# A softmax sum with half the products, and a multiply split between VectorE and Pool, in a four-layer attention kernel

## The chip, the core and the metric

The kernel runs on one core of one Trainium2 chip. The metric is the time of one launch on the device, in microseconds (us). PE is the matrix engine, VectorE (DVE in the profile), ScalarE (ACT) and Pool (POOL) are the three others that compute. SP issues most of the DMA transfers. Engines wait for each other through semaphores: counters that one engine raises when it has done something, and that another waits for. "Granted clock" is the share of its full clock that PE was given.

## The reference, cut to what matters

Four layers run one after the other, A, B, A, B. Layer A is a segmented attention that the change does not touch. Layer B is a recurrent one. It walks over 64 segments of 32 tokens, and each segment starts with 8 memory tokens that the segment before it produced, so no step can start before the step before it has ended.

```python
def _B_ref(x, mem0, Wq, Wk, Wv, Wo, seg_len):      # 2048 tokens, width 640, 32 heads of 128
    mask = (idx[:, None] < M) | (idx[:, None] >= idx[None, :])
    mem = mem0                                     # M = 8 memory tokens
    for s in range(n_seg):                         # 64 segments
        h = jnp.concatenate([mem, xs], axis=1)     # 8 + 32 = 40 tokens
        q, k, v = ...                              # three projections of h
        scores = jnp.where(mask, q @ k * scale, -1e9)
        p = _softmax(scores, axis=-1)
        o = (p @ v) @ Wo
        mem = o[:, :M, :]                          # the next step needs this
        outs.append(o[:, M:, :])
```

## The kernel before

A step s of layer B is one pass through the code below; `i4 = s % 4`. Work on heads is done in two halves b = 0 and 1, 16 heads each. The 40 keys of a head are split in two groups: 32 keys (8 older tokens and 24 of the segment), and 8 "tail" keys. A score tile holds, for each of four heads r, 56 columns: 16 columns for the tail keys (only the last 16 queries may see them) and 40 columns for the 32 keys and all 40 queries. All engines run their instructions in program order.

```python
def alloc_h(s):                                    # called for s + 1 at the start of step s
    hT[s] = hp.tile([128, NCH, 56], BF16, name="b_hT", tag="hT")
    nc.gpsimd.tensor_copy(hT[s][:, :, 0:24], xcols(s, 0, 24))         # by Pool, a step ahead
    nc.gpsimd.tensor_copy(hT[s][:, :, 32:56], xcols(s + 1, 0, 24))    # by Pool
    # ...columns 24:32, the memory tokens, come from VectorE at the end of step s - 1

def scores(b):
    t = SP[b] = ps_tile([128, 512], F32, "b_SP")
    # ...4 mask products, then 32 score products (KT is the weight, QT is streamed)
    nc.scalar.activation(out=PT[:, b]..., in_=t[:, 0:224], func=ACT.Exp, scale=SCB, **acc)

def sums(b):                                       # blk holds ones: a product with it adds over keys
    sm_ = SP[b][:, 256:480].rearrange("p (r c) -> p r c", c=56)
    for k in range(2):
        for part in range(2):
            for j in range(4):
                c0, c1 = ((16, 56), (40, 56))[k] if part == 0 else (0, 16)
                rhs = PT[:, b, :, 0:16] if k else PT[:, b, :, 40:56] if part else PT[:, b, :, 16:56]
                nc.tensor.matmul(sm_[32 * j:32 * j + 32, :, c0:c1], lhsT=blk[:, k, j],
                                 rhs=rhs, start=(k == 0 and part == 0), stop=(k == 1), ...)

def normalise(b):
    R = wk.tile([128, 4, 56], F32, name="b_R", tag="R")
    flat = R[:].rearrange("p r c -> p (r c)")
    nc.scalar.activation(out=flat, in_=SP[b][:, 256:480], func=ACT.Ln)
    nc.scalar.activation(out=flat, in_=flat, func=ACT.Exp, scale=-1.0)      # 1 / sum
    nc.vector.tensor_tensor(out=PT[:, b], in0=PT[:, b], in1=R[:], op=ALU.mult)
    if not general:
        nc.gpsimd.tensor_tensor(out=Rtot[:], in0=Rtot[:], in1=R[:, :, 16:56], op=ALU.add)
```

The order of a step, as PE gets it (`V0` and `V1` are the projections of the values, 5 parts of 4 products each; `fill` puts in products of the next tile of four segments, or deferred output products, for about so many us; `op` is the output projection):

```python
qk(Q, 0); qk(K, 0); qk(Q, 1); K1.run(2)
scores(0)
K1.run(3)
if i4 == 0 and T + 1 < NT: tail_cols(T + 1)        # Pool copies b_hx
V0.run(1); sums(0); normalise(0); V0.run(4)
scores(1)
V1.run(3)
values(0)                                          # 32 products b_OTL, weights b_Vsb and b_Vt, PT streamed
V1.run(2); sums(1)
take("act", 0, 0); take("act", 0, 1)               # ScalarE casts b_OTL to b_OTsb
normalise(1)
op.run(4); op.run(4)                               # b_OPS
fill(0.44)
values(1)
fill(0.66)
take("dve", 1, 0); take("act", 1, 1)
op.run(8)
# ...Pool copies b_OTdef; VectorE turns b_OPS into b_TM and adds it into b_hT of the next step
```

Of the kernel before, what the change touches and what calls it, by code (L numbers as in the profile page):

```python
# [18 lines left out]
F32 = mybir.dt.float32  # L19
BF16 = mybir.dt.bfloat16  # L20
ACT = mybir.ActivationFunctionType
ALU = mybir.AluOpType
# [565 lines left out]
def layer_B(nc, tc, C, W, wo_src, x_src, xb_src, x_dst, mem0, general, nsteps=64, out_bf16=False):  # L588
# [3 lines left out]
    nc = _OrdNC(tc, nc_raw, engines=ORDER_ENGINES)  # L592
    assert nsteps % 4 == 0
    NT = nsteps // 4
    with ExitStack() as ctx:
# [3 lines left out]
        wk = st  # L599
# [15 lines left out]
        blk = st.tile([128, 2, 4, 32], BF16, name="b_blk")  # L615
# [4 lines left out]
        if not general:  # L620
            Rtot = st.tile([128, 4, 40], BF16, name="b_Rtot")
# [249 lines left out]
        for s in range(nsteps):  # L871
# [32 lines left out]
            PT = wk.tile([128, 2, 4, 56], BF16, name="b_PT", tag="PT")  # L904
# [5 lines left out]
            SP = {}  # L910
# [72 lines left out]

            def sums(b):

                sm_ = SP[b][:, 256:480].rearrange("p (r c) -> p r c", c=56)
                for k in range(2):
                    for part in range(2):
                        for j in range(4):
                            c0, c1 = ((16, 56), (40, 56))[k] if part == 0 else (0, 16)  # L990
                            rhs = PT[:, b, :, 0:16] if k else PT[:, b, :, 40:56] if part else PT[:, b, :, 16:56]
                            nc.tensor.matmul(sm_[32 * j:32 * j + 32, :, c0:c1], lhsT=blk[:, k, j],
                                             rhs=rhs, start=(k == 0 and part == 0), stop=(k == 1),
                                             tile_position=(0, 32 * j), skip_group_check=True)

            def normalise(b):

                R = wk.tile([128, 4, 56], F32, name="b_R", tag="R")
                flat = R[:].rearrange("p r c -> p (r c)")
                nc.scalar.activation(out=flat, in_=SP[b][:, 256:480], func=ACT.Ln)  # L1000
                nc.scalar.activation(out=flat, in_=flat, func=ACT.Exp, scale=-1.0)
                nc.vector.tensor_tensor(out=PT[:, b], in0=PT[:, b], in1=R[:], op=ALU.mult)
                if not general:
                    nc.gpsimd.tensor_tensor(out=Rtot[:], in0=Rtot[:], in1=R[:, :, 16:56], op=ALU.add)

            def values(b):
                for jp in range(2):
# [40 lines left out]
            V0 = VPass(0)  # L1048
            V0.run(1)
            sums(0)  # L1050
            normalise(0)
            V0.run(4)
            if general:
# [10 lines left out]
            if g_need < NT:  # L1064
                ln_norm(g_need)
            V1.run(2)
            sums(1)
            take("act", 0, 0)
            take("act", 0, 1)
            normalise(1)  # L1070
            if g_need < NT:
                ln_apply(g_need)
# [3 lines left out]
            op = OPass(lambda h: OTsb[:, h, 0:32], HORDER, "b_OPS", po, "op")  # L1076
# [18 lines left out]
            if not last:  # L1095
                TM = wk.tile([128, 10, 32], F32, name="b_TM", tag="TM")
                nc.vector.transpose(out=TM[:].rearrange("p g t -> p (g t)"), in_=ops[:])
                for hf in range(2):
                    nc.vector.tensor_tensor(out=hT[s + 1][64 * hf:64 * hf + 64, :, 24:32], in0=TM[0:64, hf:10:2, 24:32],
                                            in1=TM[64:128, hf:10:2, 24:32], op=ALU.add)  # L1100
# [129 lines left out]
```

## Time and profile before

| | before |
|---|---|
| time, median of 3 runs (lowest to highest) | 2479.77 us (2478.43 to 2483.33) |
| span of the profiled run | 2479.6 us |
| PE busy | 2268.0 us, 91% |
| VectorE, Pool, ScalarE busy | 1584.5, 1014.1, 975.4 us |
| one step of layer B, median for i4 = 0, 1, 2, 3 | 13.11, 13.05, 13.30, 13.63 us |

First come lines of the page of the kernel before: the span, the busy time and number of instructions of each engine, and the DMA queue by which PE's instructions are fetched (packets, MB, share of 16 DMA engines).

```profile
span 2479.6 us, 127703 instructions
...
PE 2268.0 (91%) x57036; PEld 1309.4 (53%) x57036; DVE 1584.5 (64%) x3643; ACT 975.4 (39%) x2195; POOL 1014.1 (41%) x2333
...
q8 instruction: 448, 7.34, 1.3%
```

PE is nearly always busy, so what counts is the little time in which it is not. 448 packets with 7.34 MB are 16,384 bytes each. PE executes about 114,000 instructions here (57,036 products and as many weight loads), and 256 instructions to a packet account for nearly all the packets, so this queue is PE's.

Next, from the list of what PE waited for in the kernel before: total us, times, the longest. The list has only waits of over 150 ns, so it doesn't count every join. The word "issue" means that the profile shows nothing that PE waited for.

```profile
PE b_Qa L91 <- DVE b_hT L91: 19.5, 62, 1.2
...
PE b_OTL L91 <- issue: 5.1, 14, 0.6
...
PE b_OPSd L91 <- issue: 3.1, 6, 0.9
```

All lines say L91, because one helper records nearly every instruction; go by the names of tiles. The first line is the join between steps: PE waits for VectorE's addition into `b_hT`. The other two are waits in the midst of a group of equal products.

The timeline of the kernel before, second half of one step and the start of the next (start in us, duration in us, engine, instruction, number; in brackets the idle time before it and what ended it):

```profile
1015.92 0.39 DVE L91 TENSOR_TENSOR b_PT<-b_PT,b_R 128x224 bf16<-128x224 bf16 x1 [0.34 <-ACT b_R L91]
...
1016.03 0.63 POOL L91 TENSOR_TENSOR b_Rtot<-b_Rtot,b_R 128x160 bf16<-128x160 bf16 x1 [2.16 <-ACT b_R L91]
...
1019.29 0.40 POOL L91 COPY b_OTdef<-b_OTsb 128x256 bf16<-128x256 bf16 x1
1019.44 0.52 DVE L91 TENSOR_TENSOR b_hT<-b_TM 64x40 bf16<-64x40 f32 x2
...
1020.08 1.01 PEld L91 LDWEIGHTS <-b_hT 128*32 128x32 bf16 x24 [0.66 <-POOL b_OTdef L91]
1020.11 1.26 PE L91 MATMUL b_Qa<-b_wq,b_hT 128*32 128x512 bf16 x20 [0.20 <-DVE b_hT L91]
```

VectorE's multiply of `b_PT` ends at 1016.31. Pool's addition of `b_Rtot` starts beside it and ends at 1016.66. At the end of the step, VectorE finishes `b_hT` at 1019.96 and PE's first product of the next step starts at 1020.11.

### The profile page before, as it was taken

To read this page: it belongs to the slowest core of one execution; us is meant where nothing else is said; L and a number is where in the kernel's file an instruction comes from. 1 tells how busy PE (TensorE), PEld (TensorE's weight loads), DVE (VectorE), ACT (ScalarE), POOL (GpSimd) and SP (SyncE) were. 2 spreads that over 40 slices of the span, in tenths; PEclk is the share of its full clock that TensorE was granted. 3 is DMA by queue.
4 is the path that set the end of the run, shared out by engine and by line. 5 is a ranking of instruction groups with operands and counts; after the bars stand their busy time and mean duration, and the time that the engine had idled before them with its cause. 6 is when DMAs were issued, how large, how long until landed. Compare 5 with 4: busy or idle time off the path is not lost. (4 is left out here: it accounts for less than half of the span.)

```text
span 2479.6 us, 127703 instructions
## 1 busy us (share of the span) xinstructions
PE 2268.0 (91%) x57036; PEld 1309.4 (53%) x57036; DVE 1584.5 (64%) x3643; ACT 975.4 (39%) x2195; POOL 1014.1 (41%) x2333
## 2 busy tenths in 40 slices
PE   6888979999999999999868789699999999999997
PEld 3444435565655555556534444355555555555554
DVE  5666646666666666666556666466666666666665
ACT  4656633333333333333246566333333333333322
POOL 2334434444444444444323344344444444444442
PEclk9988979999999999999978889899999999999999
DMA  6563340111101011110032343400100000000000
GB/s 182 136 175 123 103 137 20 25 26 24 26 22 25 23 25 24 26 23 20 20 100 84 95 127 107 148 19 22 23 21 23 21 20 22 22 22 22 17 19 16
DMA packets 98864, 132.11 MB, mean 53 GB/s; under 512 B 20592, under 2 KB 84096, under 8 KB 96384
## 3 DMA queue, kind: packets, MB, share of 16 engines
q1 hardware_dynamic: 96704, 122.20, 18.2%
q8 instruction: 448, 7.34, 1.3%
q10 hardware_dynamic: 1600, 1.66, 0.2%
q14 instruction: 112, 0.92, 0.1%
HBM read 89.17 MB, written 26.21 MB: 47 GB/s over the span
## 5 line engine op out<-in xcount | busy, mean ns | idle before, releaser
L91 PEld LDWEIGHTS <-b_hT 128*32 128x32 bf16 x15520 | 409.2, 96 | 329.4 <-issue 43.3
L91 ACT ACTIVATE b_PT<-b_SP 128x224 bf16<-128x224 f32 x256 | 92.2, 360 | 789.6 <-PE b_SP L91 768.2
L91 PE MATMUL b_V<-b_wv,b_hT 128*32 128x512 bf16 x5120 | 371.2, 381 | 0.8 <-issue 0.5
L91 ACT ACTIVATE a_PT<-a_S 128x768 bf16<-128x768 f32 (+1 forms) x384 | 325.4, 892 | 80.8 <-PE a_S L91 72.4
L91 PE MATMUL b_OPS<-b_wo,b_OTsb 128*32 128x320 bf16 x8192 | 329.5, 300 | 5.4 <-DVE b_OTsb L91 5.3
L91 POOL TENSOR_TENSOR b_Rtot<-b_Rtot,b_R 128x160 bf16<-128x160 bf16 x256 | 158.0, 617 | 268.7 <-ACT b_R L91 268.4
L91 PEld LDWEIGHTS <-b_OTsb 128*32 128x32 bf16 x8192 | 200.4, 96 | 96.5 <-DVE b_OTsb L91 45.2
L91 POOL CAST b_QT<-b_TQ 128x384 bf16<-128x384 f32 x254 | 140.7, 554 | 255.4 <-DVE b_TQ L91 255.4
L91 ACT CAST b_OTsb<-b_OTL 128x320 bf16<-128x320 f32 x384 | 150.9, 428 | 217.0 <-PE b_OTL L91 188.0
L91 POOL CAST b_KT<-b_TQ 128x384 bf16<-128x384 f32 x254 | 142.6, 562 | 167.1 <-DVE b_TQ L91 167.1
L91 POOL TENSOR_SCALAR_AFFINE_SELECT a_PT<-a_PT 128x256 bf16<-128x256 bf16 x256 | 109.5, 432 | 214.7 <-ACT a_PT L91 203.5
L91 PE MATMUL b_Kb<-b_wk,b_hT 128*32 128x512 bf16 x2560 | 187.3, 381 | 0.0
L91 PE MATMUL b_Qa<-b_wq,b_hT 128*32 128x512 bf16 x2560 | 164.1, 384 | 22.7 <-DVE b_hT L91 19.5
L91 PE MATMUL b_Ka<-b_wk,b_hT 128*32 128x512 bf16 x2560 | 164.9, 384 | 0.0
L91 PE MATMUL a_PP<-a_xnT,a_wt 128*128 128x512 bf16 x560 | 160.2, 423 | 2.9 <-DVE a_t1k L91 0.8
L91 PE MATMUL b_Qb<-b_wq,b_hT 128*32 128x512 bf16 x2560 | 162.6, 380 | 0.0
L91 DVE TENSOR_TENSOR b_PT<-b_PT,b_R 128x224 bf16<-128x224 bf16 x256 | 101.8, 398 | 85.2 <-ACT b_R L91 84.9
L91 PE MATMUL a_S<-a_qk 32*128 32x512 bf16 (+3 forms) x1024 | 143.4, 322 | 7.7 <-ACT a_PT L91 6.4
L91 DVE STREAM_TRANSPOSE b_TQ<-b_Qa 128x512 f32<-128x512 f32 x128 | 91.7, 717 | 78.2 <-PE b_Qa L91 36.1
L91 DVE STREAM_TRANSPOSE b_TM<-b_OPS 128x320 f32<-128x320 f32 x126 | 65.1, 517 | 119.2 <-PE b_OPS L91 119.2
L91 DVE CAST a_qk<-a_PP 128x512 bf16<-128x512 f32 x128 | 88.0, 687 | 74.3 <-PE a_PP L91 74.3
L91 PEld LDWEIGHTS <-b_hx 128*32 128x32 bf16 x3840 | 99.6, 97 | 66.5 <-issue 10.0
(162 smaller groups left out, 4105.9 us busy)
## 6 DMA issues: line engine op xcount, KB each, us to landing
a_wt<-a_wpad SPq DMA_DIRECT2D x112, 160.0 KB
b_wo<-in_B_Wo_dram SPq DMA_DIRECT2D x8, 1280.0 KB
b_Vt<-b_Vtb SPq DMA_DIRECT2D x512, 16.0 KB
b_XO<-xres SPq DMA_DIRECT2D x256, 30.0 KB
a_wvo<-in_A_wo_dram SPq DMA_DIRECT2D x8, 800.0 KB
b_wq<-in_B_Wq_dram SPq DMA_DIRECT2D x20, 256.0 KB
b_wk<-in_B_Wk_dram SPq DMA_DIRECT2D x20, 256.0 KB
xres<-a_xo SPq DMA_DIRECT2D x16, 320.0 KB
```

What stands on the lines that cost most here:

```text
L91: r = f(*a, **k)
```

## The change

Its intent: the sum over the keys is the same for each query, whether its weight sits in the 40 columns of the 32 keys or in the 16 columns of the tail keys. The kernel before computes it twice for the last 16 queries (16 products, 352 streamed columns in each of four column groups). The change computes it once for each of the 40 queries (8 products, 224 columns) and uses the last 16 results for both. ScalarE's Ln and Exp get 160 columns instead of 224, VectorE multiplies 160 columns instead of 224, and a new multiply on Pool does the 64 tail columns beside it.

```diff
             def sums(b):
-                sm_ = SP[b][:, 256:480].rearrange("p (r c) -> p r c", c=56)
+                sm_ = SP[b][:, 256:416].rearrange("p (r c) -> p r c", c=40)
                 for k in range(2):
-                    for part in range(2):
-                        for j in range(4):
-                            c0, c1 = ((16, 56), (40, 56))[k] if part == 0 else (0, 16)
-                            rhs = PT[:, b, :, 0:16] if k else PT[:, b, :, 40:56] if part else PT[:, b, :, 16:56]
-                            nc.tensor.matmul(sm_[32 * j:32 * j + 32, :, c0:c1], lhsT=blk[:, k, j],
-                                             rhs=rhs, start=(k == 0 and part == 0), stop=(k == 1), ...)
+                    for j in range(4):
+                        nc.tensor.matmul(sm_[32 * j:32 * j + 32, :, 24 * k:40], lhsT=blk[:, k, j],
+                                         rhs=PT[:, b, :, 0:16] if k else PT[:, b, :, 16:56], start=(k == 0), stop=(k == 1), ...)

             def normalise(b):
-                R = wk.tile([128, 4, 56], F32, name="b_R", tag="R")
+                R = (wk if general else sm).tile([128, 4, 40], F32, name="b_R", tag="R")
                 flat = R[:].rearrange("p r c -> p (r c)")
-                nc.scalar.activation(out=flat, in_=SP[b][:, 256:480], func=ACT.Ln)
+                nc.scalar.activation(out=flat, in_=SP[b][:, 256:416], func=ACT.Ln)
                 nc.scalar.activation(out=flat, in_=flat, func=ACT.Exp, scale=-1.0)
-                nc.vector.tensor_tensor(out=PT[:, b], in0=PT[:, b], in1=R[:], op=ALU.mult)
+                nc.vector.tensor_tensor(out=PT[:, b, :, 16:56], in0=PT[:, b, :, 16:56], in1=R[:], op=ALU.mult)
+                nc.gpsimd.tensor_tensor(out=PT[:, b, :, 0:16], in0=PT[:, b, :, 0:16], in1=R[:, :, 24:40], op=ALU.mult)
                 if not general:
-                    nc.gpsimd.tensor_tensor(out=Rtot[:], in0=Rtot[:], in1=R[:, :, 16:56], op=ALU.add)
+                    nc.gpsimd.tensor_tensor(out=Rtot[:], in0=Rtot[:], in1=R[:], op=ALU.add)
```

(Arguments that are the same on both sides are cut as `...`. `sm` is a pool with two buffers where `wk` has one.)

More of the change, by code (lines that the diff above doesn't have):

```diff
@@ L984, in sums @@
             def sums(b):
-                sm_ = SP[b][:, 256:480].rearrange("p (r c) -> p r c", c=56)
+                sm_ = SP[b][:, 256:416].rearrange("p (r c) -> p r c", c=40)
                 for k in range(2):
-                    for part in range(2):
-                        for j in range(4):
-                            c0, c1 = ((16, 56), (40, 56))[k] if part == 0 else (0, 16)
-                            rhs = PT[:, b, :, 0:16] if k else PT[:, b, :, 40:56] if part else PT[:, b, :, 16:56]
-                            nc.tensor.matmul(sm_[32 * j:32 * j + 32, :, c0:c1], lhsT=blk[:, k, j],
-                                             rhs=rhs, start=(k == 0 and part == 0), stop=(k == 1),
-                                             tile_position=(0, 32 * j), skip_group_check=True)
+                    for j in range(4):
+                        nc.tensor.matmul(sm_[32 * j:32 * j + 32, :, 24 * k:40], lhsT=blk[:, k, j],
+                                         rhs=PT[:, b, :, 0:16] if k else PT[:, b, :, 16:56], start=(k == 0), stop=(k == 1),
+                                         tile_position=(0, 32 * j), skip_group_check=True)
             def normalise(b):
-                R = wk.tile([128, 4, 56], F32, name="b_R", tag="R")
+                R = (wk if general else sm).tile([128, 4, 40], F32, name="b_R", tag="R")
                 flat = R[:].rearrange("p r c -> p (r c)")
-                nc.scalar.activation(out=flat, in_=SP[b][:, 256:480], func=ACT.Ln)
+                nc.scalar.activation(out=flat, in_=SP[b][:, 256:416], func=ACT.Ln)
                 nc.scalar.activation(out=flat, in_=flat, func=ACT.Exp, scale=-1.0)
-                nc.vector.tensor_tensor(out=PT[:, b], in0=PT[:, b], in1=R[:], op=ALU.mult)
+                nc.vector.tensor_tensor(out=PT[:, b, :, 16:56], in0=PT[:, b, :, 16:56], in1=R[:], op=ALU.mult)
+                nc.gpsimd.tensor_tensor(out=PT[:, b, :, 0:16], in0=PT[:, b, :, 0:16], in1=R[:, :, 24:40], op=ALU.mult)
                 if not general:
-                    nc.gpsimd.tensor_tensor(out=Rtot[:], in0=Rtot[:], in1=R[:, :, 16:56], op=ALU.add)
+                    nc.gpsimd.tensor_tensor(out=Rtot[:], in0=Rtot[:], in1=R[:], op=ALU.add)
             def values(b):
```

## The prediction

> **What bounds the kernel now.** PE is busy 91% of the 2479.6 us span (the page's first part); the chain of waits is almost all PE. The change touches only layer B: 128 steps of about 13.2 us, each with two softmax sums. In the timeline, three hand-overs inside a step are not PE-bound:
> - The second group of score products starts 55 ns after VectorE's cast b_KT ends, in three steps of four (i4 = 0, 1, 2). It starts 94 ns after its mask products, against 69 ns in i4 = 3, where LayerNorm transposes on PE give VectorE time. So PE already loses 25 ns there.
> - b_OPS starts 53 ns after ScalarE's first b_OTsb cast ends, in every step; the sums before it end some 100 ns earlier.
> - The next b_Qa waits for VectorE's b_TM and b_hT.
>
> **What the change does.**
> - PE: a sum is 16 products, 352 streamed columns per column group, 155 ns from its first product to the next V product. Afterwards 8 products and 224 columns: estimated 100 ns, 53 ns less, 256 times = 13.6 us.
> - ScalarE: Ln (357 ns) and Exp (391 ns) lose 64 columns, about 50 ns each (estimate from casts: 428 ns at 320 columns, 580 at 512).
> - VectorE: the b_PT multiply, 393 ns, becomes about 326 ns (estimate, 1 ns an element).
> - Pool: a new 64-column multiply, about 300 ns alone (estimate between its 2-column add, 190 ns, and 160-column add, 485 ns). It will not really run beside VectorE: today the b_Rtot add, released with the multiply, ends 347 ns after that multiply (630 ns instead of 485). That agrees with the Trainium skill, "SBUF — State Buffer", "SBUF: two separate sides": GpSimd and a VectorE op with two SBUF inputs take the shared port pair exclusively. I expect Pool's multiply to end about 170 ns after VectorE's: together no earlier than now.
>
> **What lies on the critical path.** The multiplies have slack: values(0) starts 446 ns after its multiply, values(1) 215 to 250 ns; a wait that binds shows 53 ns (last four steps of a layer). Values start a constant 312 ns after the last 512-column product, 99 ns over its streaming; the skill ("TensorEngine Tiling (Array Packing)", "Key Properties": changing the tiling mode drains the engine) agrees. The second sum's 53 ns run into the wait for b_OTsb: nothing gained. The first sum's run into the wait for b_KT in i4 = 0, 1, 2: nothing. Only 32 steps of i4 = 3 gain: 32 x 53 ns = 1.7 us. PE's instruction-fetch pauses (about 20 us, at multiples of 128 products) may shrink by 0.5 us with 4096 PE instructions gone. Against that, in i4 = 0 Pool first copies b_hx; its multiply then ends near the start of values(0): 0 to 1.5 us lost.
>
> **Time.** About 2477.5 us; 8 in 10 within 2468 to 2485. Faster by over 2%: 0.01; within 2%: 0.98; slower: 0.01.
>
> **What would show it.** PE busy falls by some 10 us while the span hardly moves; mask to score products grows from 94 to about 147 ns in i4 = 0, 1, 2, still 55 ns after b_KT; b_OPS still 53 ns after b_OTsb; i4 = 3 steps shorter by 50 ns, the others equal; Pool's multiply ending 150 to 200 ns after VectorE's.
>
> **What would make it wrong.** If the two hand-overs move with PE, up to 14 us are gained. If Pool's multiply cannot start before VectorE's has finished, or takes over 400 ns, values(1) stalls up to 0.1 us a step: 2485 to 2490.

## More of the kernel before

Last, the chain that ended last, in order of time (start, us, what), at two places of the kernel before:

```profile
1985.77 0.21 DVE b_hT L91
1985.97 0.14 issue
1986.11 1.26 PE b_Qa L91 x20
...
2046.39 0.18 PE b_OTL L91 x12
2046.58 0.15 issue
2046.72 0.29 PE b_OTL L91 x20
```

The first three lines are the join between steps again: 0.14 us pass from the end of `b_hT` to `b_Qa`. The last three lines show a pause of 0.15 us between the 12th and the 13th of 32 equal products whose data had all been there. The 13th is the first instruction of a new block of 256 of PE's instructions.

## The result, and the profile after

| | before | after |
|---|---|---|
| time, median (lowest to highest), same rounds | 2480.36 us of 4 runs (2478.43 to 2483.33) | 2442.91 us of 4 runs (2438.73 to 2446.84) |
| ratio (95% interval) | | 0.9848 (0.9825 to 0.987) |
| span of the profiled run, granted clock | 2479.6 us, 0.957 | 2438.3 us, 0.959 |
| PE busy | 2268.0 us | 2243.2 us |
| first 60 steps of the two layers B together | 813.0 + 802.4 us | 790.7 + 789.4 us |

A ratio here is the mean time of one kernel's runs over the mean of the other's of the same rounds, so it is not quite the ratio of the medians that are quoted. The kernel after is 1.5% faster, which is still "within 2%", but 37 us faster where the prediction gave 2 us. Its time lies outside the predicted range. The output agreed with the reference, as it did in all runs that follow.

The lines that answer to those of before. From the page of the kernel after:

```profile
span 2438.3 us, 123357 instructions
...
PE 2243.2 (92%) x54926; PEld 1249.5 (51%) x54988; DVE 1582.2 (65%) x3643; ACT 946.2 (39%) x2195; POOL 1072.0 (44%) x2589
...
q8 instruction: 431, 7.06, 1.2%
...
L91 POOL TENSOR_TENSOR b_PT<-b_PT,b_R 128x64 bf16<-128x64 bf16 x256 | 104.9, 410 | 214.9 <-ACT b_R L91 190.4
...
L91 DVE TENSOR_TENSOR b_PT<-b_PT,b_R 128x160 bf16<-128x160 bf16 x256 | 104.5, 408 | 46.8 <-ACT b_R L91 28.6
```

PE has 2,048 products and as many weight loads less (the page shows 62 products too few, all of the layers A: some records are missing), and 17 packets of instructions less. VectorE's multiply, with 160 columns instead of 224, did not become cheaper on average: 408 ns against 398 ns before.

From what PE waited for in the kernel after ("issue" before `b_OPSd` is gone from the list, and little is left of "issue" before `b_OTL`):

```profile
PE b_Qa L91 <- DVE b_hT L91: 7.1, 9, 1.1
...
PE b_OTL L91 <- issue: 0.5, 2, 0.2
```

The timeline of the kernel after, the same step as above:

```profile
994.36 0.33 DVE L91 TENSOR_TENSOR b_PT<-b_PT,b_R 128x160 bf16<-128x160 bf16 x1 [0.22 <-ACT b_R L91]
994.40 0.45 POOL L91 TENSOR_TENSOR b_PT<-b_PT,b_R 128x64 bf16<-128x64 bf16 x1 [1.83 <-ACT b_R L91]
...
997.84 0.40 POOL L91 COPY b_OTdef<-b_OTsb 128x256 bf16<-128x256 bf16 x1
997.99 0.53 DVE L91 TENSOR_TENSOR b_hT<-b_TM 64x40 bf16<-64x40 f32 x2
998.58 3.36 PEld L91 LDWEIGHTS <-b_hT 128*32 128x32 bf16 x68 [0.60 <-DVE b_hT L91]
998.58 1.26 PE L91 MATMUL b_Qa<-b_wq,b_hT 128*32 128x512 bf16 x20
```

And its chain of waits at such a join:

```profile
1992.74 0.21 DVE b_hT L91
1992.95 0.04 issue
1992.99 1.26 PE b_Qa L91 x20
```

Pool's multiply starts beside VectorE's and ends at 994.85, 0.16 us after it, as predicted. The weight load of the next step is put down to VectorE, no more to Pool. And the join, 0.14 us of "issue" before, is 0.04 us now. Nothing in the change names `b_hT`.

### Where the 37 us went

I aligned both traces step by step and product by product. Two things account for nearly all of it.

**A. The join between steps.** From the end of VectorE's last addition into `b_hT` to the first `b_Qa`, the median is 147 ns before and 55 ns after, in every kind of step. Over 126 joins, 92 ns each are 11.6 us; summed from the traces, over the first 60 steps of each layer, it is 11.3 us.

In the program's list of instructions with their waits, the first weight load of `b_hT` in a step waits for VectorE and Pool before the change, and for VectorE alone after it. Pool has to be waited for because its two early copies into `b_hT` (in `alloc_h`) must be there. In the kernel after, PE has already waited for Pool's new multiply at `values`, in the same step. That multiply stands later in Pool's program than the copies, so the wait covers them, and the framework leaves the second wait out.

What a second wait looks like in the trace: PE gets a separate wait instruction for VectorE's semaphore ahead of the weight load, and the weight load carries the wait for Pool. The Trainium skill says so too ("Perfetto Trace Analysis", "Identifying Dependency Chains": an instruction that waits for several engines may get EventSemaphore instructions inserted before it). It names no cost. Traces agree and have the count: 283 such wait instructions on PE before, 31 after. About 126 of those that went stood before `b_Qa`; the other 126 stood before the first score products of a step, where `b_KT` comes from VectorE and Pool together. The cost at the join is 92 ns each. Pool had been done long before (its copies were a step old).

**B. Pauses at the ends of PE's instruction blocks.** I numbered PE's instructions in program order. The pauses all sit at one residue modulo 256, so this is where a block ends. For every such boundary I took the gap there over the median of the same gap in the other steps of the same i4. Before, 75 of 418 such boundaries show a pause, together 26.1 us. After, 18 do, together 3.2 us. That is 22.9 us. (A second count from the traces, over the 392 and 374 boundaries inside steps and from product to product, gives 25.7 and 3.8 us. So these sums are good to about 1 us.) The Trainium skill ("Runtime: NRT & Kernel Launch", "Instruction fetch mechanics") says that instructions are refilled in blocks of 16 KiB, 256 instructions, which the packets confirm (7.34 MB in 448 packets), and that the cost of crossing such a boundary is "mostly hidden". Here it was not. That the pauses are waits for instructions shows in the times: in the kernel before, at pauses of over 0.1 us, the first product after the boundary starts 1.41 us (median; nine in ten between 1.25 and 1.60) after a packet of this queue has ended. At boundaries without a pause the median is 2.6 us.

Why they shrank is inferred from the same queue. In the thirteen traces two fetches hardly ever start less than 3.3 us apart (9 of 5,666 distances; the shortest is 2.2 us, in c4_misalign). A step of 13.2 us has about 800 PE instructions, just over 3 blocks, so on average a block may take 4.2 us and there is no shortage. But from the second scores to the second values PE runs many small products, without pauses 256 instructions in 2.8 to 2.9 us before the change and in 3.0 to 3.2 us after it, and there it outruns the fetches. Without its pauses, a block of the kernel before would have taken under 3.3 us in 115 of 371 cases, and in 16 of 354 after. The change takes its 8 products and 8 weight loads out of exactly this dense stretch. The count of short blocks is a rough guide only: in my second count 51 of 78 pauses before, but 1 of 24 after, come at the end of such a block, and 66 such blocks before end without a pause. So the rate of fetching explains the direction, not each pause.

The rest is small. In the steps of i4 = 3 the first sum's 58 ns were gained, 1.8 us net. In three steps of the first layer B the kernel before lost 1.5 us to a late residual load. The layers A, whose code is the same, were about 5 us shorter in the profiled run of after. That is within the variation of single runs: outside the first 60 steps of the two layers B, the thirteen profiled runs took from 856.8 to 865.9 us (864.2 before, 858.2 after). The two spans differ by 41.3 us and the medians by 37.5. The terms add up to the spans to within some 2 us.

### The profile page after: what moved, and what is told of

The parts are those of the page before. It is cut to its first block, busy times and chain, and to the rows that moved or that the text cites. A ratio compares the mean times of both kernels' runs of the same rounds, so it can differ in the third digit from the quotient of the medians. Undisturbed runs are those within 1.5% of the kernel's fastest.

```text
span 2438.3 us, 123357 instructions
## 1 busy us (share of the span) xinstructions
PE 2243.2 (92%) x54926; PEld 1249.5 (51%) x54988; DVE 1582.2 (65%) x3643; ACT 946.2 (39%) x2195; POOL 1072.0 (44%) x2589
## 5 line engine op out<-in xcount | busy, mean ns | idle before, releaser
L91 PEld LDWEIGHTS <-b_hT 128*32 128x32 bf16 x15520 | 380.8, 96 | 343.8 <-DVE b_hT L91 65.9
L91 PE MATMUL b_V<-b_wv,b_hT 128*32 128x512 bf16 x5120 | 361.4, 381 | 0.0
L91 POOL TENSOR_TENSOR b_PT<-b_PT,b_R 128x64 bf16<-128x64 bf16 x256 | 104.9, 410 | 214.9 <-ACT b_R L91 190.4
L91 PE MATMUL a_PP<-a_xnT,a_wt 128*128 128x512 bf16 x505 | 147.3, 405 | 9.7 <-issue 5.5
L91 DVE TENSOR_TENSOR b_PT<-b_PT,b_R 128x160 bf16<-128x160 bf16 x256 | 104.5, 408 | 46.8 <-ACT b_R L91 28.6
L91 DVE CAST b_Vsb<-b_V 128x512 bf16<-128x512 f32 x128 | 88.5, 691 | 67.9 <-PE b_SP L91 53.9
```

The source lines that it names most:

```text
L91: r = f(*a, **k)
```

## The experiments

Two theories were on the table after the result. Theory A+B: the gain is the dropped wait at the join, plus fewer pauses of the instruction fetch. Rival: PE's saved work (53 ns of products a sum, 13.6 us in all) comes through after all, together with something else. A second rival, for B: the pauses depend on where the boundaries happen to fall, and the change moved them by luck.

| run | from | median us | ratio (95%) | pauses, us | `b_hT` to `b_Qa`, ns |
|---|---|---|---|---|---|
| before | | 2476.91 to 2482.8 | 1 | 26.1 | 147 |
| after | | 2442.91 | 0.9848 | 3.2 | 55 |
| e1_sums_only | after | 2465.79 | 0.9957 (0.9939 to 0.9975) | 8.3 | 147 |
| e2_pool_only | before | 2457.91 | 0.9922 (0.9903 to 0.994) | 17.0 | 55 |
| e3_hT_scalar | before | 2471.94 | 0.9981 (0.9963 to 1.0) | 23.4 | 55 |
| e4_hT_late | after | 2452.81 | 0.9908 (0.9885 to 0.9931) | 2.5 | 147 |
| p1_shift | after | 2445.5 | 0.9851 (0.9832 to 0.987) | 4.0 | 54 |
| p3_wide | after | 2446.77 | 0.9855 (0.9838 to 0.9871) | 3.4 | 54 |
| d1_before_shift | before | 2473.39 | 0.9974 (0.9957 to 0.9991) | 25.3 | 146 |
| c1_reorder | after | 2419.28 | 0.9748 (0.9731 to 0.9766) | 9.1 | 54 |
| c2_fill | c1 | 2407.02 | 0.9697 (0.9681 to 0.9713) | 14.7 | 91 |
| c3_align | c2 | 2406.09 | 0.9691 (0.9675 to 0.9707) | 2.8 | 91 |
| c4_misalign | c2 | 2415.17 | 0.9735 (0.9713 to 0.9757) | 9.6 | 91 |

Each ratio is to the kernel before in the same rounds. The first four runs were one call (before: 2476.91), d1, c3 and c4 another (2480.6), the other four a third (2482.8), each on another chip; across calls the ratios compare better than the times. In c2, c3 and c4 the moved products fill the wait before `b_Qa`, so `b_hT` no longer ends it. The pauses of e3_hT_scalar are those of the second count; by the same count the others agree with the table within 1.1 us. An account to a few us is the most that these runs allow: d1_before_shift is 7 us faster than the kernel before with the same pauses and the same join, and nothing here explains that.

### e1_sums_only: the new sums, no work for Pool

```diff
-                nc.gpsimd.tensor_tensor(out=PT[:, b, :, 0:16], in0=PT[:, b, :, 0:16], in1=R[:, :, 24:40], op=ALU.mult)
+                nc.vector.tensor_tensor(out=PT[:, b, :, 0:16], in0=PT[:, b, :, 0:16], in1=R[:, :, 24:40], op=ALU.mult)
```

> The change without its Pool multiply: 8 products a sum, 160-column R, but VectorE scales both parts. Theory (two causes: PE's double wait for b_hT, and pauses of PE at every 256th instruction, fewer with fewer PE instructions): the wait for VectorE and Pool before b_Qa stays, so b_hT to b_Qa stays 147 ns; the pauses, 26 us in the kernel before, fall to about 3 to 6 us; i4 = 3 steps gain 53 ns. Time about 2454 to 2458, a gain of about 24 us. Rival A (the time came from Pool taking work off VectorE): no gain, about 2478 or more. Rival B (all of it is PE work saved, 13.6 us): about 2466.

Measured: 2465.79 us, 11 us less than before, where 2454 to 2458 was expected. The join is back at 147 ns, as theory A says: Pool's multiply is what removes the wait. The pauses are 8.3 us, more than the kernel after has but far fewer than before. The trace shows one cost that I had not counted: VectorE's second multiply comes ahead of its later casts, so the second half of `b_OPS` starts 14 to 40 ns later and `b_hT` ends 22 ns later in the steps of i4 = 2 and 3, about 4 us in all. In the trace the first 60 steps of the two layers B are 15.4 us shorter than before. By the time alone this run would fit the rival; p3_wide below decides against that.

### e2_pool_only: the old sums, and the split multiply

```diff
-                nc.vector.tensor_tensor(out=PT[:, b], in0=PT[:, b], in1=R[:], op=ALU.mult)
+                nc.vector.tensor_tensor(out=PT[:, b, :, 16:56], in0=PT[:, b, :, 16:56], in1=R[:, :, 16:56], op=ALU.mult)
+                nc.gpsimd.tensor_tensor(out=PT[:, b, :, 0:16], in0=PT[:, b, :, 0:16], in1=R[:, :, 0:16], op=ALU.mult)
```

> The kernel before with its 16 products a sum and 224-column R, but the tail columns scaled by Pool. Theory: PE now waits for Pool at the values, so its wait for Pool before b_Qa falls away: b_hT to b_Qa 55 ns instead of 147, 126 times, 11.6 us; the pauses at the 256th instructions stay about 20 to 26 us, as PE's instructions stay. Time about 2466 to 2470. Rival A (Pool taking work off VectorE is the cause): about 2443. Rival B (PE work saved): no gain, 2478 to 2482.

Measured: 2457.91 us, 19 us less than before, with not one product taken from PE. That is more than expected. The list of PE's waits in this run has

```profile
PE b_Qa L91 <- DVE b_hT L91: 7.9, 14, 1.1
```

so the join is as short as in the kernel after. The other part was new to me: the pauses fell from 26.1 to 17.0 us, though PE has the same number of products and weight loads as before. What went are PE's separate wait instructions. So the split multiply gives the whole of A and a part of B; the new sums alone (e1) give nothing of A and the larger part of B.

### e3_hT_scalar: before, with the early copies moved from Pool to ScalarE

```diff
-            nc.gpsimd.tensor_copy(hT[s][:, :, 0:24], xcols(s, 0, 24))
+            nc.scalar.copy(hT[s][:, :, 0:24], xcols(s, 0, 24))
-                nc.gpsimd.tensor_copy(hT[s][:, :, 32:56], xcols(s + 1, 0, 24))
+                nc.scalar.copy(hT[s][:, :, 32:56], xcols(s + 1, 0, 24))
```

> The kernel before, nothing of the change, only the two copies of x into b_hT moved from Pool to ScalarE, which PE has waited for later in its order anyway. Theory: b_Qa's weights wait for VectorE alone, b_hT to b_Qa 55 ns instead of 147, 11.6 us gained, pauses as in the kernel before: 2466 to 2470. Rival (the 92 ns come from something else in the change, say Pool's or VectorE's timing): 147 ns stay and the time stays about 2480.

This takes the Pool wait away by another way: PE waits for ScalarE anyhow, later in ScalarE's program. The join fell to 55 ns, as expected, and the pauses to 23.4 us. In the trace the first 60 steps of the two layers B are 14.0 us shorter; the join gives 11.3 us of it, fewer pauses some 2 us. But the time fell by 5 us only (at most 9 by the interval), to just above the expected range, where the join alone should give 11.6; the profiled run and the timed runs do not agree here. The mechanism at the join is confirmed, the size of its effect on the whole is not confirmed by this run, and where the rest went stays open. Against e2_pool_only this run shows one thing more. It keeps the wait instructions before the first score products, and e2 has none. Yet a step of i4 = 3 takes 13.54 us in both, so those cost nothing measurable by themselves: an extra wait instruction is not worth 92 ns wherever it stands.

### e4_hT_late: after, with the early copies issued late on Pool

The two copies keep their engine and their data, but are issued after `normalise(1)`, so they stand in Pool's program after the multiply that PE waits for.

```diff
         def alloc_h(s):
             hT[s] = hp.tile([128, NCH, 56], BF16, name="b_hT", tag="hT")
+            if s == 0:
+                fill_h(s)
+
+        def fill_h(s):
             nc.gpsimd.tensor_copy(hT[s][:, :, 0:24], xcols(s, 0, 24))
...
             normalise(1)
+            if not last:
+                fill_h(s + 1)
```

> The changed kernel with the copies of x into b_hT moved on Pool from the start of a step to after the second multiply, so that PE's earlier wait for Pool no longer covers them and b_Qa's weights wait for VectorE and Pool again. Theory: b_hT to b_Qa 147 ns again, 11.6 us lost against the changed kernel, pauses still small (3 to 6 us): about 2452 to 2457. Rival: no loss, about 2443.

Measured: 2452.81 us, 10 us more than the kernel after (15 us by the ratios; 12.7 us in the first 60 steps of the two layers B), and the pauses stay small, 2.5 us. The chain of this run at the join, and then the line from the list of PE's waits:

```profile
2002.73 0.21 DVE b_hT L91
2002.94 0.14 issue
2003.08 1.48 PE b_Qa L91 x20
```

```profile
PE b_Qa L91 <- DVE b_hT L91: 19.9, 68, 1.2
```

The same copies, done long before they are needed in both kernels (2.8 us before `b_Qa` in this one), cost 92 ns a step as soon as their place in Pool's program brings the second wait back. This is the cleanest proof of A: one thing changed, and the time moved by about what 126 times 92 ns predict.

### p3_wide: after, with all the streamed columns put back

Still 8 products a sum, but they stream 320 columns instead of 224, so PE has most of the old sum's work with the new number of instructions.

```diff
-                sm_ = SP[b][:, 256:416].rearrange("p (r c) -> p r c", c=40)
+                sm_ = SP[b][:, 256:512].rearrange("p (r c) -> p r c", c=64)
...
-                        nc.tensor.matmul(sm_[32 * j:32 * j + 32, :, 24 * k:40], lhsT=blk[:, k, j],
-                                         rhs=PT[:, b, :, 0:16] if k else PT[:, b, :, 16:56], ...)
+                        nc.tensor.matmul(sm_[32 * j:32 * j + 32, :, 40 * k:56 + 8 * k], lhsT=blk[:, k, j],
+                                         rhs=PT[:, b, :, 0:24] if k else PT[:, b, :, 0:56], ...)
```

(Ln then reads the 40 columns that count, out of 64.)

> The changed kernel with its 8 products a sum, but 320 streamed columns instead of 224 (the kernel before streams 352): the same PE instructions, most of the PE work given back, 40 ns a sum, 10 us in all. Theory: that work is hidden behind the waits for b_KT and b_OTsb except in i4 = 3 (1.3 us); pauses about 3 us; time 2443 to 2446. Rival (PE work saved is what paid): about 2453.

Measured: 2446.77 us, ratio 0.9855 against 0.9848 of after. The sum took 138 ns again instead of 98. Steps of i4 = 0, 1 and 2 kept their length within 3 ns, and only those of i4 = 3 became 39 ns longer. PE's saved work is not what paid, and the rival falls. This part of the prediction was right.

### p1_shift and d1_before_shift: the same programs, with their blocks moved

A few tiny products, executed once ahead of the first layer B, move every later block boundary: by 128 instructions in the kernel after (p1), by 64 in the kernel before (d1). In d1 the loop runs 32 times.

```diff
+        if not general and not out_bf16:
+            dummy = ps_tile([32, 16], F32, "b_dummy")
+            for i in range(64):
+                nc.tensor.matmul(dummy[:], lhsT=C.identb[:, 0:32], rhs=C.identb[:, 0:16], start=(i == 0), stop=(i == 63))
```

> The changed kernel with 64 tiny products (128 PE instructions, under 2 us) once, before the steps of the first layer B: every step is the same program, only moved by half a block of 256 PE instructions, in both layers B. Theory (PE pauses where its 256-instruction blocks end inside the dense part of a step, so place matters as well as number): in the runs so far this step's worst places are those that the shift now reaches; pauses 8 to 12 us instead of 3, time 2447 to 2453. Rival (only the number of PE instructions of a step matters): pauses 3 us, time about 2444.

> The kernel before with 32 tiny products (64 PE instructions) once before the steps of the first layer B, which moves every later step by a quarter of a block of 256 PE instructions. Theory (the pauses come from 16 more products a step in its dense part; place only spreads them): pauses 15 to 30 us, time 2472 to 2486. Rival (the kernel before only had unlucky places): pauses 3 to 8 us, time about 2460.

The kernel before keeps 25.3 us of pauses, as expected; its list of PE's waits still has

```profile
PE b_OTL L91 <- issue: 4.1, 13, 0.4
```

The kernel after keeps 4.0 us, where I had expected 8 to 12. So at these places at least its few pauses are not luck, and the second rival falls on both sides. Four steps have 3,202 PE instructions before and 3,066 after. Neither is a multiple of 256, so the boundaries walk through the step anyhow.

### c1_reorder and c2_fill: can the saved 53 ns be had?

The prediction said that both sums run into waits (the first for VectorE's `b_KT`, the second for ScalarE's `b_OTsb`). If that is so, putting products between the sum and the wait should bring the gain. c1 moves parts of the projection V1: one before `scores(1)`, one before `values(0)`, and three after it; Pool's `b_hx` copy goes behind `normalise(0)`.

```diff
-            if i4 == 0 and T + 1 < NT:
-                tail_cols(T + 1)
             V0 = VPass(0)
             V0.run(1)
             sums(0)
             normalise(0)
+            if i4 == 0 and T + 1 < NT:
+                tail_cols(T + 1)
             V0.run(4)
...
-            scores(1)
             V1 = VPass(1)
-            V1.run(3)
+            V1.run(1)
+            scores(1)
+            V1.run(1)
             values(0)
...
-            V1.run(2)
+            V1.run(3)
             sums(1)
```

c2 is c1 with less filling ahead of `values(1)`:

```diff
-            fill(0.44)
+            fill(0.3 if i4 == 0 else 0.22)
```

> The changed kernel with the second V pass spread: 1 part before the second scores, 1 before values(0), 3 after (before: 0, 3, 2), b_hx copied after the first multiply. It fills the two PE waits that the change only lengthened: 84 ns before the score products (i4 = 0, 1, 2) and about 160 ns before b_OPS. Theory: 250 ns a step in i4 = 0, 1, 2, 165 ns in i4 = 3, about 29 us, less what denser PE instructions give back in pauses (0 to 8 us): 2414 to 2424. Rival (the waits only move on to the values, whose multiplies then bind): 2435 to 2443.

> c1 with one part of the tail work moved from before values(1) to the end of the step, where PE idles about 170 ns before b_Qa for the transposed output. Theory: up to 20 us less than c1, minus pauses: 2395 to 2412. Rival (values(1) then waits for Pool's multiply, or b_hT binds all the same): as c1 or slower.

Measured: 2419.28 us and 2407.02 us, both inside what was expected. The timeline of the kernel after, at the second sum of one step and the second scores of the next:

```profile
993.22 0.27 PE L91 MATMUL b_SP<-b_PT,b_blk 128*32 128x160 bf16 x8
...
993.47 1.27 PE L91 MATMUL b_OPS<-b_wo,b_OTsb 128*32 128x320 bf16 x32
...
1004.38 0.26 PE L91 MATMUL b_SP<-b_mask,c_identb 128*32 128x160 bf16 x4
...
1004.54 0.37 PE L91 MATMUL b_SP<-b_QT,b_KT 128*32 128x40 bf16 x32
```

and of c1_reorder at the same products, with the sum and the output projection after it:

```profile
994.72 0.26 PE L91 MATMUL b_SP<-b_mask,c_identb 128*32 128x160 bf16 x4
...
994.79 0.39 PE L91 MATMUL b_SP<-b_QT,b_KT 128*32 128x40 bf16 x32
...
996.32 0.27 PE L91 MATMUL b_SP<-b_PT,b_blk 128*32 128x160 bf16 x8
...
996.42 1.26 PE L91 MATMUL b_OPS<-b_wo,b_OTsb 128*32 128x320 bf16 x32
```

From mask to score products it is 0.16 us in after and 0.07 us in c1 (medians 153 and 69 ns); from the second sum to `b_OPS` it is 0.25 us in after (993.22 to 993.47 in its timeline) and 0.10 us in c1. In c1 both hand-overs now follow PE: in i4 = 0, 1, 2 the score products start 187 ns after `b_KT` where it was 55, and `b_OPS` 100 to 112 ns after the first `b_OTsb` cast where it was 53. These two waits were the place where the sums' gain stayed, as the prediction had it. But c1 fills the whole of both waits, which were there in part before the change. No run has the new order with the old sums, so how much of its gain needs the new sums is not shown. c2 fills a third wait, the one before `b_Qa`, with products moved to the end of the step. c2_fill is 3% below the kernel before and beats both kernels. It also pays something back: a denser step has more pauses, 9.1 us in c1 and 14.7 us in c2, against 3.2.

### c3_align and c4_misalign: fixing the boundary in the step

If four steps have a multiple of 256 PE instructions, the boundaries stay at the same places in each group of four steps. In both runs c2 got 3 tiny products in each first sum of i4 = 0, which makes it 3,072 = 12 x 256. A few products ahead of each layer then choose the place: 12 of them put a boundary just ahead of a group that waits anyhow (c3); 76 put it into the dense stretch (c4).

```diff
+        if not general:
+            dummy = ps_tile([128, 16], F32, "b_dummy")
+            for i in range(102 if out_bf16 else 12):      # c4: 76
+                nc.tensor.matmul(dummy[32 * (i % 4):32 * (i % 4) + 32, :], lhsT=C.identb[:, 0:32], rhs=C.identb[:, 0:16], ...)
...
+                if not general and b == 0 and i4 == 0:
+                    for j in range(3):
+                        nc.tensor.matmul(SP[b][32 * j:32 * j + 32, 416:432], lhsT=blk[:, 0, j], rhs=PT[:, b, 0, 16:32], ...)
```

> c2 with 3 tiny products more in every fourth step, so that four steps are 3072 = 12 x 256 PE instructions and the block ends stay at one place, and 12 and 102 tiny products before the two layers, which set that place 14 instructions before the group of four steps. There the runs before showed no pauses with the changed kernel's program. Theory: pauses fall from 15 us in c2 to 0 to 4 us, the extra products cost about 3 us: 2393 to 2402. Rival (place does not matter): pauses 15 us, about 2410.

> As c3, but with 76 instead of 12 products before the first layer B: the block ends stay half a block away, 142 instructions before the group, where c2 paused 450 to 800 ns in four steps. Theory: pauses 15 to 24 us, 2408 to 2420, some 15 us above c3. Rival: no difference to c3 beyond 2 us.

c3's pauses fell to 2.8 us, as expected, but its time equals that of c2, 2406.09 us, where 2393 to 2402 was expected. c4 is 9 us slower than c3, where some 15 were expected. So the place of the boundary does matter in a dense program, 9 us here, even though it did not in the kernel after. c4's 9.6 us of pauses are counted too low: they stand at the same place in each group of four steps, so the median that I subtract contains some of them.

What ate c3's gain, in the profiled run at least, is read from that run. First come three lines of its timeline at the start of a step of i4 = 2, then a line of its list of PE's waits:

```profile
501.50 1.01 DVE L91 TENSOR_TENSOR b_XO<-b_OPS,b_XO 64x320 f32<-64x320 f32 x2 [2.20 <-DMA b_XO<-xres]
...
502.54 0.72 DVE L91 STREAM_TRANSPOSE b_TQ<-b_Qa 128x512 f32<-128x512 f32 x1
...
503.31 0.62 PE L91 MATMUL b_Kb<-b_wk,b_hT 128*32 128x512 bf16 x8 [0.50 <-DVE b_TQ L91]
```

```profile
PE b_Kb L91 <- DVE b_TQ L91: 2.5, 6, 0.6
```

The residual rows of the segment (`b_XO`) came late, VectorE stood 2.2 us at its addition, and everything behind it in VectorE's program came late. The load is late because SP waits for the store from the same buffer to land (61.1 us in 62 waits in c3, 41.5 us in 51 in c2). Six steps of the first layer B are 1.05 to 1.42 us longer for it, 7.4 us in all; without them the profiled run would have been at 2399 us, as expected. I don't know whether the timed runs had the same; the fastest of the four was 2400.51 us. No run tried a second buffer for `b_XO`, so that stays open.

### What the runs say together about the pauses

| pauses, us | wait instructions at `b_Qa` and `b_KT` | only one of them | none |
|---|---|---|---|
| 16 products a sum | 26.1 (before), 25.3 (d1) | 23.4 (e3: at `b_KT`) | 17.0 (e2) |
| 8 products a sum | 8.3 (e1) | 2.5 (e4: at `b_Qa`) | 3.2 (after), 3.4 (p3), 4.0 (p1) |

Reading down, 8 products a sum fewer take away 13 to 18 us. Reading across, the dropped wait instructions take away 4 to 9 us. Most of that goes with those at `b_KT` (about 6 us from e3 to e2, 5 to 6 us from e1 to e4), under 3 us with those at `b_Qa`. Both directions are measured, but no run drops the wait instructions at `b_KT` and changes nothing else. That a PE which stops at a separate wait instruction loses what it could have run ahead is only argued; no run here looks into its sequencer.

## Why the prediction was wrong, point by point

The prediction gave 2477.5 us, 8 in 10 within 2468 to 2485. Measured were 2442.91 us. The class, within 2%, was right.

| term | predicted, us | measured, us |
|---|---|---|
| second sum's 53 ns | 0 | 0 |
| first sum's 53 ns | -1.7 (i4 = 3 only) | -1.8 (i4 = 3 only) |
| Pool's multiply ahead of `values(0)` | 0 to +1.5 | 0 |
| instruction-fetch pauses | -0.5 | -22.9 |
| join between steps | 0 (no term) | -11.3 |
| late residual loads in before | 0 (no term) | -1.5 |
| layers A, same code | 0 | about -5 in the spans, within the spread of single runs |

Right:

- PE's saved work stays off the critical path. The products of a sum went from 155 to 98 ns, PE's busy time fell by 25 us (some 10 predicted), and the waits behind the sums took it up: mask to score products grew from 94 to 153 ns in i4 = 0, 1, 2 while the score products still start 55 ns after `b_KT`, and `b_OPS` still starts 53 ns after the first `b_OTsb` cast. p3_wide put work back at no cost in i4 = 0, 1, 2, and c1_reorder moved other work into the waits and gained.
- Pool does not really run beside VectorE. Its multiply ends 165 ns after VectorE's (predicted 170) and takes 445 ns where it waits, 302 ns alone (predicted 300). The Trainium skill's exclusive lock ("SBUF — State Buffer", "SBUF: two separate sides") agrees with that.
- `values(0)` and `values(1)` did not move for it.

Wrong:

- "The next b_Qa waits for VectorE's b_TM and b_hT." This is the first step that failed. The wait was listed, but as one for VectorE only, and as one that the change leaves alone. 92 ns of its 147 ns were the second wait, for Pool's copies of a step earlier, and the change removed that by making PE wait for Pool at another place. The profile's line of the weight load named Pool; the prediction went by the product's line, which named VectorE. e4_hT_late shows it.
- "PE's instruction-fetch pauses (about 20 us, at multiples of 128 products) may shrink by 0.5 us with 4096 PE instructions gone." This is the second, and the larger. The pauses, their place and about their size were seen. The scaling was wrong. It took the pauses as nearly proportional to the number of all instructions, 4% of which went. They arise in the dense stretch of a step, and the instructions went from just there; the blocks that PE needs in under 3.3 us fell from 115 to 16. The term measured 22.9 us: by e1_sums_only the fewer products give most of it, and by e2_pool_only the dropped wait instructions can take away 9 us.
- "i4 = 3 steps shorter by 50 ns, the others equal." The median step of each kind became at least 88 ns shorter, because the join is in each of them.
- The VectorE multiply: 393 ns were to become 326. It takes 325 where it starts alone. In i4 = 0, 1, 2 the first one of a step overlaps Pool's cast of `b_KT` and takes 541 ns (in the timeline of after it shows as 0.54 us from 1004.48), so its mean is 408. The prediction had the lock in one direction only. It cost nothing, as there is slack before `values(0)`.

## What to carry to other kernels

Before costing a change by engine time, list for each engine's important joins which semaphores they wait for, and ask which waits the change makes redundant or brings in: here a producer that had finished long ago still cost 92 ns at every join, because it made a second wait there (at another place in the same step a second wait cost nothing measurable by itself). Where PE runs hundreds of small products in a row, count its instructions in each such stretch and look for pauses at every 256th: here 16 fewer in a dense stretch gave far more than their own time, and the program that was made denser paid some of it back in pauses. When the saved work of an engine vanishes into a wait behind it, moving independent work into that wait can recover it; here that, with a third wait filled as well, gave some 36 us more than the change itself.

## What the Trainium skill lacked or had wrong

- "Runtime: NRT & Kernel Launch", "Instruction fetch mechanics", has the 256 instructions of a block right, but calls the crossing "mostly hidden". Here 75 of 418 crossings paused PE, 26.1 us of 2480 in all. The page gives no rate of fetching; in these traces 9 of 5,666 distances between fetches are under 3.3 us, and in the kernel before PE's small products use up 256 instructions in 2.8 to 2.9 us.
- "Perfetto Trace Analysis", "Identifying Dependency Chains", names the extra wait instructions of an instruction with several waits, but not their cost. Here one costs 92 ns at a join on the critical path, another nothing measurable by itself, and 283 of them against 31 go with 4 to 9 us more of fetch pauses. No page says that a wait elsewhere, on a later instruction of the same engine, makes such a wait unnecessary; e2_pool_only and e4_hT_late show it.
- "SBUF — State Buffer", "SBUF: two separate sides": the page gives no times for the exclusive lock; these runs agree with it and have some. Pool's 64-column multiply, 302 ns alone, ends 165 ns after VectorE's. The other way round, VectorE's 160-column multiply, 325 ns alone, takes 541 ns where it overlaps Pool's cast of `b_KT`, and ends 175 ns after it. So the second instruction ends some 140 to 150 ns sooner than if it had begun only when the first ended; the page does not say that.
